# When may the first store start? Splitting the last load of a streaming kernel and releasing two large stores by its landing

## Chip, cores, metric

One core of a Trainium2 chip. The metric is device time in microseconds, median of the runs; all runs told here are with a granted clock of 1.0. Not all ran on one chip: the first four experiments ran on chip 0, the four at 28 and 4, at 10 and 22 rows and with the early whole load on chip 5, the other four on chip 4, each beside runs of before on the same chip (for the first pair the record names no chip). A kernel is best judged by its ratio to before of the same rounds; medians from different chips are compared only roughly. The profile's span is some 1.3 us shorter than the device time of the same execution, so spans are compared with spans and times with times.

## The reference

```python
B, S, D = 1024, 16, 512          # all bf16
def reference(x, y, gamma):      # x, y: [1024, 16, 512], gamma: [512]
    return x + gamma * y
```

That is 16384 rows of 1 KB in each of x, y and the result: 33.6 MB in, 16.8 MB out, one multiply and one add for each element.

## The kernel before

Each of the 128 partitions owns 128 consecutive rows. They are worked in four pieces of 32 rows. SP issues the loads in a fixed order, ACT issues the stores, VectorE multiplies and adds in place in `y_sb`. x has room for two pieces only, so its third and fourth load wait for the first and second add.

```python
PIECES = [32, 32, 32, 32]
X_AT = [0, 32, 0, 32]
X_AFTER = [-1, -1, 0, 1]         # the add that frees the place

SP = [('x', 0), ('y', 0), ('x', 1), ('y', 1), ('y', 2), ('x', 2), ('y', 3), ('x', 3)]
ACT = [('g',), ('s', 0, 0, 2), ('s', 1, 1, 2), ('s', 2, 2, 2), ('s', 3, 3, 3)]
                                  # store, from piece, to piece, after which add
# ... cut ...
    for c in range(n):
        yt = y_sb[:, piece(c), :]
        _take(s_y[c], 16, nc.vector)
        nc.vector.tensor_tensor(out=yt, in0=yt, in1=gamma_sb..., op=MULT).then_inc(s_dve, 1)
        _take(s_x[c], 16, nc.vector)
        _take(s_dve, 1, nc.vector)
        nc.vector.tensor_tensor(out=yt, in0=x_tile(c), in1=yt, op=ADD).then_inc(s_add, 1)
```

All stores, even of the first two pieces, wait for the third add (`2` in the last place). So loads and stores follow one another and hardly overlap.

## Time and profile before

| | |
|---|---|
| time, first three runs | 120.30, 120.31, 120.99 us |
| span of the profiled run | 119.5 us |
| DMA engines | q1 (loads) 66.4% + q10 (stores) 32.5% of the span |
| VectorE | 59% busy, eight passes of 8.69 us |

To read what follows: a *packet* is one record of the profile, here the contiguous run of one partition. A transfer has *landed* when the last of the 16 DMA engines has signalled the end of its part. A line of a *stretch* gives start and end and length in us, the busy time (and number of instructions) of TensorE, its weight load, VectorE and GpSimd, the granted clock, the busy share of the DMA engines and their GB/s. A packet is counted whole in the stretch in which it starts, so the share can pass 1. A line of the *order of time* gives start, duration, engine, line and tiles. The prediction below shows such lines of the kernel before, and why stretches are multiples of the packet time.

### The profile page before, as it was taken

To read this page: it belongs to the slowest core of one execution; us is meant where nothing else is said; L and a number is where in the kernel's file an instruction comes from. 1 tells how busy PE (TensorE), PEld (TensorE's weight loads), DVE (VectorE), ACT (ScalarE), POOL (GpSimd) and SP (SyncE) were. 2 spreads that over 40 slices of the span, in tenths; PEclk is the share of its full clock that TensorE was granted. 3 is DMA by queue.
4 is the path that set the end of the run, shared out by engine and by line. 5 is a ranking of instruction groups with operands and counts; after the bars stand their busy time and mean duration, and the time that the engine had idled before them with its cause. 6 is when DMAs were issued, how large, how long until landed. Compare 5 with 4: busy or idle time off the path is not lost. (4 is left out here: it accounts for less than half of the span.)

```text
span 119.5 us, 84 instructions
## 1 busy us (share of the span) xinstructions
PE 0.6 (0%) x1; PEld 0.1 (0%) x1; DVE 70.2 (59%) x10; POOL 0.2 (0%) x4
## 2 busy tenths in 40 slices
PE   0100000000000000000000000000000000000000
PEld 0000000000000000000000000000000000000000
DVE  0100000699999289999999999999999600000000
POOL 0000000000000000000000000000000000000000
DMA  7989898998998989898989999898989898989995
GB/s 208 494 373 504 351 526 351 384 493 351 384 493 351 526 351 526 351 515 362 493 384 471 406 428 450 384 493 351 526 351 526 351 526 351 515 362 471 406 471 230
DMA packets 1730, 50.33 MB, mean 421 GB/s; under 512 B 193, under 2 KB 194, under 8 KB 194
## 3 DMA queue, kind: packets, MB, share of 16 engines
q1 hardware_dynamic: 1152, 33.55, 66.4%
q10 hardware_dynamic: 578, 16.78, 32.5%
HBM read 33.56 MB, written 16.78 MB: 421 GB/s over the span
## 5 line engine op out<-in xcount | busy, mean ns | idle before, releaser
L115 DVE TENSOR_TENSOR y_sb<-y_sb,gamma_sb 128x16384 bf16<-128x16384 bf16 x4 | 34.8, 8688 | 18.4 <-DVEq L22 18.4
L120 DVE TENSOR_TENSOR y_sb<-x_sb,y_sb 128x16384 bf16<-128x16384 bf16 x4 | 34.8, 8692 | 0.6
L109 DVE CAST gamma_sb<-gamma_ps 128x512 bf16<-128x512 f32 x1 | 0.7, 692 | 3.4 <-DVEq L22 3.4
L104 DVE MEMSET ones_row<- 1x128 bf16 x1 | 0.2, 165 | 2.0 <-PEq L38 2.0
L107 PE MATMUL gamma_ps<-gamma_row,ones_row 1*128 1x512 bf16 x1 | 0.6, 580 | 4.8 <-PEq L22 4.8
L107 PEld LDWEIGHTS gamma_ps<-gamma_row,ones_row 1*128 1x128 bf16 x1 | 0.1, 100 | 4.8 <-issue 4.8
L149 POOL MEMSET const-bfloat16-1.0<- 128x1 bf16 x1 | 0.1, 101 | 0.0
L149 POOL MEMSET const-uint8-127<- 128x1 uint8 x1 | 0.1, 101 | 0.0
L149 POOL MEMSET const-float32-0.0<- 128x1 f32 x1 | 0.1, 98 | 0.2 <-issue 0.2
L149 POOL MEMSET const-float32-1.0<- 128x1 f32 x1 | 0.1, 98 | 0.0
## 6 DMA issues: line engine op xcount, KB each, us to landing
x_sb<-in_x_dram SPq DMA_DIRECT2D x4, 4096.0 KB, 21.5
y_sb<-in_y_dram SPq DMA_DIRECT2D x4, 4096.0 KB, 35.4
out_dram<-y_sb ACTq DMA_DIRECT2D x4, 4096.0 KB, 23.8
gamma_row<-in_gamma_dram ACTq DMA_DIRECT2D x1, 1.0 KB
```

Source lines behind the costliest of these rows:

```text
L104: nc.vector.memset(ones_row, 1.0).then_inc(s_ones, 1)
L107: nc.tensor.matmul(gamma_ps, ones_row, gamma_row, start=True, stop=True).then_inc(s_ps, 1)
L109: nc.vector.tensor_copy(out=gamma_sb, in_=gamma_ps).then_inc(s_dve, 1)
L115: nc.vector.tensor_tensor(out=yt, in0=yt, in1=gamma_sb[:, None, :].to_broadcast([P, PIECES[c], D]), op=MULT).then_inc(s_dve, 1)
L120: nc.vector.tensor_tensor(out=yt, in0=x_tile(c), in1=yt, op=ADD).then_inc(s_add, 1)
L149: nc = _bacc.Bacc("TRN2", target_bir_lowering=False, num_devices=1)
```

## The change

Its intent: the first store may go when most of the last load has landed, so that the engines pass from loads to stores without a gap and without overlap. The last load of x is cut into 22 and 10 rows. TensorE waits for the first part and passes the news to ACT (`s_go`) and to VectorE (`s_rel`). Two stores of 64 rows (64 KB per partition) take the place of four of 32.

```diff
-SP = [('x', 0), ('y', 0), ('x', 1), ('y', 1), ('y', 2), ('x', 2), ('y', 3), ('x', 3)]
-ACT = [('g',), ('s', 0, 0, 2), ('s', 1, 1, 2), ('s', 2, 2, 2), ('s', 3, 3, 3)]
+SP = [('x', 0, 32, 0), ('y', 0, 32), ('x', 32, 64, 32), ('y', 32, 64), ('y', 64, 96), ('x', 64, 96, 0), ('y', 96, 128), ('x', 96, 118, 32), ('x', 118, 128, 54)]
+ACT = [('g',), ('s', 0, 64), ('s', 64, 128)]
+RELEASE = ('x', 96, 118, 32)
 # ... cut: bookkeeping of rows instead of pieces ...
+            if kind == "s" and not went:
+                _take(s_go, 1, eng)
+                went = True
 # ... cut ...
+    _take(s_load[RELEASE], 16, nc.tensor)
+    nc.tensor.sem_inc(s_go, 1)
+    nc.tensor.sem_inc(s_rel, 1)
 # ... cut ...
+                if w == RELEASE:
+                    _take(s_rel, 1, nc.vector)
+                else:
+                    _take(s_load[w], 16, nc.vector)
```

More of the change, by code (lines that the diff above doesn't have):

```diff
@@ L6 @@
 PIECES = [32, 32, 32, 32]
-X_AT = [0, 32, 0, 32]
-X_AFTER = [-1, -1, 0, 1]
-SP = [('x', 0), ('y', 0), ('x', 1), ('y', 1), ('y', 2), ('x', 2), ('y', 3), ('x', 3)]
-ACT = [('g',), ('s', 0, 0, 2), ('s', 1, 1, 2), ('s', 2, 2, 2), ('s', 3, 3, 3)]
-EARLY = [('x', 0), ('y', 0), ('g',)]
+SP = [('x', 0, 32, 0), ('y', 0, 32), ('x', 32, 64, 32), ('y', 32, 64), ('y', 64, 96), ('x', 64, 96, 0), ('y', 96, 128), ('x', 96, 118, 32), ('x', 118, 128, 54)]
+ACT = [('g',), ('s', 0, 64), ('s', 64, 128)]
+EARLY = (2, 1)
+RELEASE = ('x', 96, 118, 32)
+DVE = [('m', 0), ('a', 0), ('m', 1), ('a', 1), ('m', 2), ('a', 2), ('m', 3), ('a', 3)]
 MULT, ADD = mybir.AluOpType.mult, mybir.AluOpType.add
@@ L56 @@
     y_sb = nc.alloc_sbuf_tensor("y_sb", [P, rows, D], dt).ap()
-    x_rows = max(a + r for a, r in zip(X_AT, PIECES))
+    x_loads = [w for w in SP + ACT if w[0] == "x"]
+    y_loads = [w for w in SP + ACT if w[0] == "y"]
+    stores = [w for w in SP + ACT if w[0] == "s"]
+    for loads in (x_loads, y_loads, stores):
+        assert sum(w[2] - w[1] for w in loads) == rows
+    x_rows = max(w[3] + w[2] - w[1] for w in x_loads)
     x_sb = nc.alloc_sbuf_tensor("x_sb", [P, x_rows, D], dt).ap()
@@ L62, with meets, pieces_of, x_at @@
     s_gamma, s_ones, s_ps, s_dve = sem("s_gamma"), sem("s_ones"), sem("s_ps"), sem("s_dve")
-    s_x = [sem(f"s_x{c}") for c in range(n)]
-    s_y = [sem(f"s_y{c}") for c in range(n)]
-    s_add, s_end, s_out = sem("s_add"), sem("s_end"), sem("s_out")
-    def piece(a, b=None):
-        return slice(starts[a], starts[(a if b is None else b) + 1])
-    def x_tile(c):
-        return x_sb[:, X_AT[c] : X_AT[c] + PIECES[c], :]
-    early, stores = [], 0
-    def ring(eng, what, known=-1):
-        nonlocal stores
-        for w in what:
-            kind, args = w[0], w[1:]
-            need = X_AFTER[args[0]] if kind == "x" else args[2] if kind == "s" else -1
+    s_load = {w: sem("s_" + "_".join(map(str, w[:2]))) for w in x_loads + y_loads}
+    s_add, s_go, s_rel, s_end, s_out = sem("s_add"), sem("s_go"), sem("s_rel"), sem("s_end"), sem("s_out")
+    added = [a for kind, *a in DVE if kind == "a"]
+    order = {a[0]: k for k, a in enumerate(added)}
+    def meets(a, b, c, d):
+        return a < d and c < b
+    def pieces_of(a, b):
+        return [c for c in range(n) if meets(starts[c], starts[c + 1], a, b)]
+    def x_at(row):
+        return next(w[3] + row - w[1] for w in x_loads if w[1] <= row < w[2])
+    def frees(w):
+        old = x_loads[: x_loads.index(w)]
+        old = [v for v in old if meets(v[3], v[3] + v[2] - v[1], w[3], w[3] + w[2] - w[1])]
+        return [c for v in old for c in pieces_of(v[1], v[2])]
+    early = []
+    def ring(eng, what, n_early):
+        known, went = 0, False
+        for k, w in enumerate(what):
+            kind = w[0]
+            need = frees(w) if kind == "x" else pieces_of(w[1], w[2]) + list(w[3:]) if kind == "s" else []
+            need = max((order[c] + 1 for c in need), default=0)
+            if kind == "s" and not went:
+                _take(s_go, 1, eng)
+                went = True
             if need > known:
-                eng.wait_ge(s_add, need + 1)
+                eng.wait_ge(s_add, need)
                 known = need
@@ L86, in ring @@
             elif kind == "x":
-                c = args[0]
-                i = eng.dma_start(out=x_tile(c), in_=xv[:, piece(c), :]).then_inc(s_x[c], 16)
+                to = x_sb[:, w[3] : w[3] + w[2] - w[1], :]
+                i = eng.dma_start(out=to, in_=xv[:, w[1] : w[2], :]).then_inc(s_load[w], 16)
             elif kind == "y":
-                c = args[0]
-                i = eng.dma_start(out=y_sb[:, piece(c), :], in_=yv[:, piece(c), :])
-                i.then_inc(s_y[c], 16)
+                r = slice(w[1], w[2])
+                i = eng.dma_start(out=y_sb[:, r, :], in_=yv[:, r, :]).then_inc(s_load[w], 16)
             else:
-                r = piece(args[0], args[1])
+                r = slice(w[1], w[2])
                 i = eng.dma_start(out=ov[:, r, :], in_=y_sb[:, r, :]).then_inc(s_out, 16)
-                stores += 1
-            if w in EARLY:
+            if k < n_early:
                 early.append(i.ins)
-    ring(nc.sync, SP)
-    ring(nc.scalar, ACT)
+    ring(nc.sync, SP, EARLY[0])
+    ring(nc.scalar, ACT, EARLY[1])
     nc.vector.memset(ones_row, 1.0).then_inc(s_ones, 1)
@@ L110, with need @@
     _take(s_dve, 1, nc.vector)
-    for c in range(n):
-        yt = y_sb[:, piece(c), :]
-        _take(s_y[c], 16, nc.vector)
-        nc.vector.tensor_tensor(
-            out=yt, in0=yt, in1=gamma_sb[:, None, :].to_broadcast([P, PIECES[c], D]), op=MULT
-        ).then_inc(s_dve, 1)
-        _take(s_x[c], 16, nc.vector)
-        _take(s_dve, 1, nc.vector)
-        nc.vector.tensor_tensor(out=yt, in0=x_tile(c), in1=yt, op=ADD).then_inc(s_add, 1)
+    _take(s_load[RELEASE], 16, nc.tensor)
+    nc.tensor.sem_inc(s_go, 1)
+    nc.tensor.sem_inc(s_rel, 1)
+    landed, open_mults = set(), 0
+    def need(loads, c):
+        for w in loads:
+            if w not in landed and meets(starts[c], starts[c + 1], w[1], w[2]):
+                if w == RELEASE:
+                    _take(s_rel, 1, nc.vector)
+                else:
+                    _take(s_load[w], 16, nc.vector)
+                landed.add(w)
+    for kind, *args in DVE:
+        c = args[0]
+        yt = y_sb[:, starts[c] : starts[c + 1], :]
+        if kind == "m":
+            need(y_loads, c)
+            g = gamma_sb[:, None, :].to_broadcast([P, PIECES[c], D])
+            nc.vector.tensor_tensor(out=yt, in0=yt, in1=g, op=MULT).then_inc(s_dve, 1)
+            open_mults += 1
+        else:
+            need(x_loads, c)
+            if open_mults:
+                _take(s_dve, open_mults, nc.vector)
+                open_mults = 0
+            at = x_at(starts[c])
+            xt = x_sb[:, at : at + PIECES[c], :]
+            nc.vector.tensor_tensor(out=yt, in0=xt, in1=yt, op=ADD).then_inc(s_add, 1)
     nc.scalar.sem_inc(s_end, 1)
@@ L125 @@
     _take(s_add, n, nc.sync)
-    _take(s_out, 16 * stores, nc.sync)
+    _take(s_out, 16 * len(stores), nc.sync)
     main = nc.main_func.blocks[0].instructions
```

## The prediction

> **What bounds the kernel now**
>
> I read the page first, its engine and queue parts, because a kernel of two elementwise passes over 50 MB is either bound by VectorE or by the DMA engines, and the change touches both.
>
> ```profile
> span 119.5 us, 84 instructions
> PE 0.6 (0%) x1; PEld 0.1 (0%) x1; DVE 70.2 (59%) x10; POOL 0.2 (0%) x4
> ...
> q1 hardware_dynamic: 1152, 33.55, 66.4%
> q10 hardware_dynamic: 578, 16.78, 32.5%
> HBM read 33.56 MB, written 16.78 MB: 421 GB/s over the span
> ```
>
> VectorE works 59% of the span. The load queue q1 and the store queue q10 together fill 66.4 + 32.5 = 98.9% of the 16 DMA engines' time. So the DMA engines are the bound, and the only idle time that is left to win is about 1.1%, or 1.3 us.
>
> The second view is a cut of the span into stretches. A packet here is one partition's 32 KB and takes about 1.21 us, so I chose stretches of about eight packets (one transfer of 4.19 MB); a stretch that does not fit whole packets shows false ups and downs such as those in the 40 slices.
>
> ```profile
> 41.80:51.50 9.70, 0.00 (x0) 0.00 (x0) 9.19 (x2) 0.00 (x0) 1.00 1.00 432
> 51.50:61.20 9.70, 0.00 (x0) 0.00 (x0) 9.70 (x2) 0.00 (x0) 1.00 1.00 432
> 61.20:70.90 9.70, 0.00 (x0) 0.00 (x0) 9.55 (x2) 0.00 (x0) 1.00 1.00 432
> 70.90:80.55 9.65, 0.00 (x0) 0.00 (x0) 9.65 (x2) 0.00 (x0) 1.00 1.01 435
> 80.55:90.20 9.65, 0.00 (x0) 0.00 (x0) 9.50 (x2) 0.00 (x0) 1.00 1.01 435
> 90.20:99.86 9.66, 0.00 (x0) 0.00 (x0) 4.37 (x1) 0.00 (x0) 1.00 1.01 434
> 99.86:109.50 9.64, 0.00 (x0) 0.00 (x0) 0.00 (x0) 0.00 (x0) 1.00 1.01 435
> ```
>
> The last column is GB/s. The reader is to see that loads (up to 80 us) run at 432 and stores (from 80 us) at 435, and that nothing dips between. The handover itself, in stretches of one packet:
>
> ```profile
> 77.60:78.80 1.20, 0.00 (x0) 0.00 (x0) 1.20 (x1) 0.00 (x0) 1.00 1.01 437
> 78.80:80.00 1.20, 0.00 (x0) 0.00 (x0) 1.20 (x1) 0.00 (x0) 1.00 1.01 437
> 80.00:81.20 1.20, 0.00 (x0) 0.00 (x0) 1.20 (x1) 0.00 (x0) 1.00 1.02 437
> 81.20:82.40 1.20, 0.00 (x0) 0.00 (x0) 1.20 (x1) 0.00 (x0) 1.00 1.01 437
> ```
>
> The third view is the order of time around the handover, which says when VectorE and the store issues happen.
>
> ```profile
> 59.72 0.33 SPq L88 DMA_DIRECT2D x_sb<-in_x_dram  x1
> 68.44 8.69 DVE L120 TENSOR_TENSOR y_sb<-x_sb,y_sb 128x16384 bf16<-128x16384 bf16 x1
> 77.05 8.68 DVE L115 TENSOR_TENSOR y_sb<-y_sb,gamma_sb 128x16384 bf16<-128x16384 bf16 x1
> 77.17 4.06 ACTq L95 DMA_DIRECT2D out_dram<-y_sb  x3
> 85.88 8.69 DVE L120 TENSOR_TENSOR y_sb<-x_sb,y_sb 128x16384 bf16<-128x16384 bf16 x1
> ```
>
> The third add ends at 77.05 and releases three stores at 77.17. The trace's single packets complete the picture: the last load packets end between 80.09 and 80.42, engine by engine, and on each engine the first store packet starts within 10 ns of that, after the load's semaphore write. No store packet runs before a load packet. The last store packets end at 118.81 to 119.15 and their landing, 0.36 us later, ends the span. So the chain that counts is: first packet at 0.99 us, 24 load-sized packets less their slow start to 80.1, then 32 store packets of 1.208 us (38.7 us), then 0.36 us of landing. The chain of waits on the page ends at the fourth add and stops there, since it does not follow DMA; it is not the bound.
>
> **What the Trainium skill says**
>
> "DMA: Bandwidth & Descriptors", section "Where 436 GB/s comes from": the 16 ports carry 435.2 GB/s at most. The trace agrees: 432 and 435 above. Store packets of 32768 bytes each took 1213 ns and follow one another every 1.208 us, which is 27.1 GB/s for one engine. There is no rate left to win. The same page, "Issuing engines are not separate DMA queues": transfers from SP and from ACT run on the same 16 engines. The trace agrees, since q1 and q10 share 98.9% of one pool. The same page, "Queues, rings and completion order": each engine takes its rows in turn, a packet at a time. The trace of before neither confirms nor refutes this for the stores, since the first store packet starts exactly where loads end. "Perfetto Trace Analysis", section "DMA Instruction — HWDGE (DVE, Sync)": the issue seen in the profile does not contain the movement. The trace agrees: the first store's issue takes 0.37 us, its first packet starts 2.92 us after the issue starts, and it lands 13.4 us after it.
>
> **The change part by part**
>
> 1. *The front is untouched.* The first eight loads have the same order, sizes and waits (the reuse of x's two halves still waits for the first and second add). Cost 0. The slow start, where the first packets take 1.8 to 2.1 us and not 1.21, stays.
>
> 2. *The last load is split into 22 and 10 rows.* Eight packets of 32 KB per engine become eight of 22 KB (22528 / 27.1 GB/s = 0.83 us) and eight of 10 KB (0.38 us). The bytes are the same. Added: eight packets and one semaphore write of about 10 ns per engine. I give it 0 to 0.1 us.
>
> 3. *Four stores become two.* Packets of 32 KB become packets of 64 KB (if they are not cut in two). A back-to-back store packet costs 1.208 us against 32768 / 27.2 GB/s = 1.205 us at the ceiling, so a packet's own overhead is about 3 ns; 16 packets fewer on each engine give 0.05 us. Two semaphore writes fewer give 0.02 us. Call it -0.05 us.
>
> 4. *The release moves from the third add to a landing.* By the packets, loads end on the engines at 80.09 (earliest) to 80.42 (latest). The 10-row part is the last eight small packets of each engine, 8 x 0.378 = 3.02 us, so the 22-row part ends on the slowest engine at 80.42 - 3.02 = 77.40. In before, the last load landed at 59.72 + 21.1 = 80.84, which is 0.42 us after its last packet. So the part lands at 77.82. TensorE takes a semaphore 0.03 us after it is there and needs 0.05 us for it (its waits of before are 51 ns); two increments and ACT's own take follow. I estimate 0.2 us for the relay, so ACT issues at 78.0, where before it issued at 77.17. The release is 0.85 us *later*, not earlier; the second add, which the first store also needs, is long done (59.7).
>
> 5. *What the handover costs.* In before, 2.92 us pass from issue to first store packet, but the first load at the start of the span needed only 0.99 us. The difference can be a real delay of the path, or the packets already committed on the engine. If it is the second, descriptors arrive at about 79.0, while 10 KB loads still have a microsecond to go: the engines have no gap, and at most a few 64 KB store packets (2.42 us each) slip ahead of the last 10 KB loads. Cost on the engines 0.
>
> 6. *VectorE and the second store.* x's last 10 rows land at 80.84, or 2.4 to 4.8 us later if one or two store packets cut in. The fourth multiply ends at 85.73, so the fourth add still starts at about 85.9 and ends at 94.6, where the second store is issued. The first store's 8.39 MB (16 x 1.208 = 19.3 us) keep the engines busy to 99.4. The second store is there 4.8 us ahead, against 0.99 to 2.9 us that it needs: no gap.
>
> Sum: 0.05 - 0.05 + 0 = 0, so the span stays 119.5 and the time stays at the 120.3 of before.
>
> **The rivals**
>
> *A gap at the handover.* If the 2.92 us are a fixed delay of the path, the first store packet starts at 78.0 + 2.92 = 80.9, and engines idle 0.5 to 0.85 us. The time becomes 120.8 to 121.1. For it: the gamma load, also issued by ACT, needed 2.95 us from issue to packet, nearly the same number. Against it: gamma too waited behind a packet in flight (it began as that packet ended), so it shows only an upper bound. I give this rival 3 in 10.
>
> *A gain from clean separation or larger packets.* If the split keeps loads and stores apart where before mixed them, stores would flow faster. Against it: before did not mix them in its profiled run, and runs at 99 to 100% of the ceiling. In runs that went otherwise (one of the three took 120.99) it might help by some tenths: 120.0.
>
> *The late rows delay VectorE.* If four or more store packets get ahead of the last load packets on some engine, the fourth add starts over 4.9 us late and the second store could leave a gap. Four packets are 9.7 us, so the add ends at 99.4 and the engines run dry for 1 to 3 us: 121.3 to 123.3. At most two or three small loads can be left when the stores arrive, so I give it 1 in 20.
>
> *64 KB runs are cut badly or are slower to HBM.* Nothing in this trace shows a packet over 32 KB. A few per cent on 38.7 us would be over 1 us. I give it 1 in 30.
>
> **Range and chances**
>
> No gap gives 120.3, a gap gives 121.0: 0.7 x 120.3 + 0.3 x 121.0 = 120.5, and the chance of a small gain takes off 0.1. I predict 120.4 us. Before itself spread from 120.3 to 120.99. The range of 119.8 to 121.1 holds both main cases. Within 2% means 117.9 to 122.7: a gain of 2.4 us needs twice the idle time that exists, so faster has 1 in 100; slower needs one of the last two rivals, 3 in 100.
>
> **What would show it**
>
> In stretches of the changed kernel, 432 to 435 GB/s on both sides of 80 us shows steps 2 and 3 right. The first ACT store issue at about 78.0 shows step 4. A stretch without a dip between 78 and 83 us shows step 5; a hole of half a microsecond there, the first rival. The start of the last add at 85.9 shows step 6; a later start with VectorE waiting shows the third rival. A store packet that takes clearly more than 2.42 us would make step 3 wrong. The prediction fails if stores run at another rate than 435 GB/s, or if DMA idles over 1 us anywhere after 5 us.

## The result and the profile after

The changed kernel took 120.12 us (median of 6, 120.08 to 120.14) against 120.46 us of before (median of 6, 120.24 to 120.99). The ratio is 0.9966 with a 95% interval of 0.9944 to 0.9988. Ratios here are the mean time of one kernel's fast runs over that of the other's of the same rounds, so not quite the ratio of the medians. The change is "same" at the 2% level, but the gain of 0.3% is clear of noise, and the changed kernel is steadier.

The page of the changed kernel, its span and queues:

```profile
span 118.8 us, 88 instructions
...
q1 hardware_dynamic: 1296, 33.56, 66.1%
q10 hardware_dynamic: 290, 16.78, 32.6%
HBM read 33.56 MB, written 16.78 MB: 424 GB/s over the span
```

The packets changed as intended (q1 1152 to 1296, q10 578 to 290), and the engines are as full as they were. Loads run at 432 GB/s and stores at 435 as before, which the prediction had named as its first sign (stretches of eight packets, of 32 KB and of 64 KB):

```profile
50.90:60.60 9.70, 0.00 (x0) 0.00 (x0) 9.70 (x2) 0.00 (x0) 1.00 1.00 432
82.00:101.30 19.30, 0.00 (x0) 0.00 (x0) 11.63 (x2) 0.00 (x0) 1.00 1.00 435
```

The order of time around the handover in the changed kernel:

```profile
58.93 0.81 SPq L110 DMA_DIRECT2D x_sb<-in_x_dram  x2
67.65 8.69 DVE L162 TENSOR_TENSOR y_sb<-x_sb,y_sb 128x16384 bf16<-128x16384 bf16 x1
76.26 8.68 DVE L153 TENSOR_TENSOR y_sb<-y_sb,gamma_sb 128x16384 bf16<-128x16384 bf16 x1
77.42 16.73 ACTq L116 DMA_DIRECT2D out_dram<-y_sb  x2
85.09 8.69 DVE L162 TENSOR_TENSOR y_sb<-x_sb,y_sb 128x16384 bf16<-128x16384 bf16 x1
```

The store is issued 1.1 us after the third add (67.65 + 8.69 = 76.34) now and not right behind it. Single packets show the rest: engine by engine the last load packet ends between 79.19 and 79.64, and the first store packet starts within 0.01 us of that. The fourth add follows the multiply without a wait.

But the two profiles can't be subtracted from each other. The 0.7 us between the spans arose much earlier, in code that the change doesn't touch. The same stretches of six packets each, first of before, then of the changed kernel (the last column is GB/s):

```profile
12.10:19.40 7.30, 0.00 (x0) 0.00 (x0) 0.00 (x0) 0.00 (x0) 1.00 1.01 431
19.40:26.70 7.30, 0.00 (x0) 0.00 (x0) 4.64 (x1) 0.00 (x0) 1.00 1.04 417
26.70:34.00 7.30, 0.00 (x0) 0.00 (x0) 7.15 (x2) 0.00 (x0) 1.00 0.90 373
34.00:41.30 7.30, 0.00 (x0) 0.00 (x0) 5.59 (x1) 0.00 (x0) 1.00 1.01 431
```

```profile
12.10:19.40 7.30, 0.00 (x0) 0.00 (x0) 0.00 (x0) 0.00 (x0) 1.00 1.00 431
19.40:26.70 7.30, 0.00 (x0) 0.00 (x0) 4.76 (x1) 0.00 (x0) 1.00 1.00 431
26.70:34.00 7.30, 0.00 (x0) 0.00 (x0) 7.15 (x2) 0.00 (x0) 1.00 1.00 431
34.00:41.30 7.30, 0.00 (x0) 0.00 (x0) 5.47 (x1) 0.00 (x0) 1.00 1.00 431
```

In the profiled run of before the load packets between 15 and 39 us took up to 1.42 us and not 1.21; summed up, 0.9 us for each engine. This "slow stretch" hits some runs and not others. A measure that leaves it out is needed: the time **from the landing of the last y load to the end** (the last landing of a store), in which the whole handover lies. By it, before had 119.51 - 71.12 = 48.39 us and the changed kernel 118.74 - 70.38 = 48.36. By this pair alone the change would do nothing, and the gain of 0.3% would be an accident of slow stretches. The experiments show that this is not the whole truth.

### The profile page after: what moved, and what is told of

Read it like the earlier page. It is cut to its first block, busy times and chain, and to the rows that moved or that the text cites. A ratio compares the mean times of both kernels' runs of the same rounds, so it can differ in the third digit from the quotient of the medians.

```text
span 118.8 us, 88 instructions
## 1 busy us (share of the span) xinstructions
PE 0.6 (0%) x1; PEld 0.1 (0%) x1; DVE 70.2 (59%) x10; POOL 0.2 (0%) x4
## 3 DMA queue, kind: packets, MB, share of 16 engines
q1 hardware_dynamic: 1296, 33.56, 66.1%
```

## The experiments

All outputs are right. The theories: **A**, the gain is chance, from the slow stretch. **B**, one part of the change (release or store size) gains. **C**, the rewritten program text misses the slow stretch. After the first four: **D**, a store issued while loads are still in flight disturbs them, and the landing avoids this by its time. **E**, the small packets of the split load make the handover steady, whoever releases.

### The changed kernel once more

No edit. 

> The changed kernel, unaltered, once more. Theory A (the change is worth under 0.1 us by itself, and the gap of 0.34 us between the medians comes from a slow stretch of load packets that some runs meet between 15 and 39 us, in code that the change does not touch): about 120.1 in most runs, but now and then a run of 120.5 to 121.0 like before. Theory B (the larger stores or the release by a landing make it faster and steadier): 120.1 in every run, before again 120.2 to 121.0. Theory C (the rewritten program, in another order of semaphores and instructions, misses the slow stretch): as B.

Measured: 120.08 us (120.00 to 120.28), before in the same rounds 120.36 (120.14 to 121.20, 11 runs), ratio 0.9965 (0.9938 to 0.9992). The gain repeats. The profiled run, the slowest of them with 120.28, did have a mild slow stretch, so the change doesn't prevent that; C in its strict form falls.

### Only the larger stores

```diff
-... ('x', 96, 118, 32), ('x', 118, 128, 54)]
-ACT = [('g',), ('s', 0, 64), ('s', 64, 128)]
+... ('x', 96, 128, 32)]
+ACT = [('g',), ('s', 0, 64, 2), ('s', 64, 128)]   # first store after the third add
+# no s_go, no s_rel: TensorE's three lines are left out
```

> Only the stores of 64 KB per partition; the last load of x is whole again and the third add releases the first store, as in before. Theory A: the stores gain 0.09 us and the load gains back the 0.1 us of the split, so 120.0 in runs without the slow stretch. Theory B with the release as the cause: 120.3 and more with the spread of before. Theory C: 120.0 in every run.

Measured: 120.39 us (120.01 to 121.10), ratio 0.9993: before's time and before's spread. So store size alone shows no gain, though the interval (0.9958 to 1.0028) is wide. In its trace the store is issued at 76.19, and the load packets that start at 77.34 to 77.67 on all 16 engines take 1.31 to 1.88 us; those that follow take 1.213 again.

### Only the split and the release

```diff
-ACT = [('g',), ('s', 0, 64), ('s', 64, 128)]
+ACT = [('g',), ('s', 0, 32), ('s', 32, 64), ('s', 64, 96), ('s', 96, 128)]
```

> Only the split and the release by the landing; the stores are four of 32 KB per partition again. Theory A: 0.09 us longer than the changed kernel, 120.2. Theory B with the larger stores as the cause: 120.3 and more, with the spread of before. Theory C: 120.2 in every run.

Measured: 120.19 us (120.10 to 120.39), ratio 0.9975 (0.9949 to 1.0002). The gain seems to be largely here, though the interval just reaches 1: of theory B split and release stay. Most of the 0.1 us that it is behind the changed kernel is the larger stores' share (0.08 us by the profiles, see below). From the last y landing to the end it took 48.47 us.

### Neither part, in the new program text

The four stores and the whole last load, the first store after the third add: the schedule of before.

```diff
-... ('x', 96, 118, 32), ('x', 118, 128, 54)]
-ACT = [('g',), ('s', 0, 64), ('s', 64, 128)]
+... ('x', 96, 128, 32)]
+ACT = [('g',), ('s', 0, 32, 2), ('s', 32, 64), ('s', 64, 96), ('s', 96, 128)]
+# no s_go, no s_rel
```

> Neither part: the loads, stores and waits of before, written by the program text of the changed kernel. Theory A: 120.1 to 120.2 where no slow stretch is met, 120.5 to 121.0 where one is, so like before. Theory B: like before, median 120.4, spread of 0.7. Theory C: 120.1 to 120.2 in every run.

Measured: 120.38 us (120.22 to 120.85), ratio 0.9992: before again, so C is out. The profiled run had no slow stretch, so it shows the handover of before's schedule alone. From the last y landing to the end: 48.87 us, 0.40 more than with split and release. The loss is in its load packets between 76.7 and 79.0 us, which took up to 1.81 us. That is theory D: the store was issued at 76.26, with three microseconds of loads ahead. But the first profile of before, issued as early (6.0 us after the last y landing in both), shows no slow packet there. So the loss comes in some runs and not in others.

### The split, but the third add releases

```diff
-ACT = [('g',), ('s', 0, 64), ('s', 64, 128)]
+ACT = [('g',), ('s', 0, 64, 2), ('s', 64, 128)]
+# no s_go, no s_rel
```

> The split of the last load and the stores of 64 KB, but the third add releases the first store again (at about 76.2 us instead of 77.4). Theory D (a store that is issued about 3 us before the loads end disturbs the load packets still in flight and costs 0.3 to 0.7 us in many runs; the release by the landing avoids it by its time): median 120.3 to 120.5, with runs up to 121, like the stores alone. Theory E (the small packets of the split load make the handover steady, whatever releases the stores): 120.1, all runs within 0.2 us.

Measured: 120.22 us (120.11 to 120.47), ratio 0.9995 (0.9972 to 1.0017). Between the two theories' numbers. The profiled run took 48.86 us from the last y landing to the end, as much as without the split, and its 10 KB load packets from 77.96 on took up to 0.67 us and not 0.39, so D for the profile; two of six runs took 120.47, none more. The split alone gains nothing.

### The whole load, the release by the third add but late

```diff
-    _take(s_load[RELEASE], 16, nc.tensor)
-    nc.tensor.sem_inc(s_go, 1)
-    nc.tensor.sem_inc(s_rel, 1)
+    nc.tensor.wait_ge(s_add, 3)
+    for k in range(2):               # about 1 us of idle work
+        late = nc.alloc_psum_tensor(f"late_ps{k}", [P, D], mybir.dt.float32).ap()
+        i = nc.tensor.matmul(late, ones_row, gamma_row, start=True, stop=True)
+    i.then_inc(s_go, 1)
```

The last load is whole, the stores are of 64 KB.

> The last load whole, stores of 64 KB, released by the third add with about 1.1 us of delay (two idle matmuls on TensorE), so that they are issued at about 77.4, as in the changed kernel, with no split and no landing. Theory D: 120.0 to 120.1, nearly as steady as the changed kernel. Theory E: 120.3 to 120.5 with runs up to 121.

Measured: 120.43 us (119.92 to 120.66), ratio 1.0002 (0.9976 to 1.0029). The handover is as D says: the store is issued at 77.47, every load packet after 75 us takes 1.21 to 1.28 us, and the stretch from the last y landing to the end is 48.53 us. But the times are not steady: three of six runs lie at 120.57 to 120.66. The profiled run (120.29) had a mild slow stretch before 70 us; the slower three were not profiled. For the time of a whole run D fails here: with the changed kernel's issue time it is no faster than before, nor than the split with the early release of the same rounds (120.22).

### No split, the landing of the whole load releases

```diff
-... ('x', 96, 118, 32), ('x', 118, 128, 54)]
-RELEASE = ('x', 96, 118, 32)
+... ('x', 96, 128, 32)]
+RELEASE = ('x', 96, 128, 32)
```

> No split: the landing of the whole last load releases the stores. The loads' last packets end at about 79.2 to 79.6, land at 80.1, and the relay takes 0.37 us, so the store is issued at 80.5. If issue to first packet takes 1.77 us, as in the changed kernel, the first store packet starts at 82.3, the engines idle 2.9 us and the time is 122.9. If it takes 0.99 us, as the first load of the span did on idle engines, the gap is 2.1 us and the time is 122.1. If the 2.9 us of before were fixed: 124.0.

Measured: 121.92 us (121.84 to 122.29), ratio 1.0139. The issue in order of time, and the stretches around it:

```profile
80.41 0.37 ACTq L116 DMA_DIRECT2D out_dram<-y_sb  x1
```

```profile
76.80:79.20 2.40, 0.00 (x0) 0.00 (x0) 2.40 (x1) 0.00 (x0) 1.00 0.92 396
79.20:81.20 2.00, 0.00 (x0) 0.00 (x0) 2.00 (x1) 0.00 (x0) 1.00 0.00 0
81.20:83.60 2.40, 0.00 (x0) 0.00 (x0) 2.40 (x1) 0.00 (x0) 1.00 1.02 437
```

The reader is to see the hole: no data packet started between 79.2 and 81.2. The first store packet starts at 81.27, 0.86 us after the issue. So the path from issue to packet costs 0.86 us on idle engines; the rest of the 2.92 us of before and of the 1.77 us of the changed kernel passed while load packets ran on the engines. The split is worth some 1.9 us (50.24 us from the last y landing to the end, against 48.36) *against this way of releasing*.

### The split at 28 and 4 rows: later

```diff
-... ('x', 96, 118, 32), ('x', 118, 128, 54)]
-RELEASE = ('x', 96, 118, 32)
+... ('x', 96, 124, 32), ('x', 124, 128, 60)]
+RELEASE = ('x', 96, 124, 32)
```

> The split moved to 28 and 4 rows, so the release comes later. The last load packets end at 79.2 to 79.6; four rows are 1.21 us of an engine, so the first part lands at about 78.8, the relay of 0.37 us makes it 79.2 for the issue, and with the 0.88 us that the whole landing showed from issue to packet on idle engines the first store packet starts at 80.1. Idle about 0.7 us: 120.7 to 120.8. If the 1.77 us of the changed kernel were the delay: 121.5.

Measured: 120.69 us (120.59 to 120.72), ratio 1.0027. Issue at 79.21, first store packet at 80.08: again 0.86 us, and the gap as worked out. This also fixes the size of the tail: landing to issue (0.35 us) plus issue to packet (0.86 us) plus last packet to landing (about 0.44 us) make 1.7 us; ten rows, 3.1 us of an engine, hide it with something to spare.

### The split at 10 and 22 rows: earlier

```diff
-... ('x', 96, 118, 32), ('x', 118, 128, 54)]
-RELEASE = ('x', 96, 118, 32)
+... ('x', 96, 106, 32), ('x', 106, 128, 42)]
+RELEASE = ('x', 96, 106, 32)
```

> The split moved to 10 and 22 rows, so the release comes early: landing at 73.4, issue at 73.8, store descriptors on the engines at about 74.7 with five to six load packets of 22 KB still to go. If each engine takes turns, a packet from each queue, every one of them waits for a store packet of 2.42 us: the last load lands at 92 to 94, the fourth add ends at 101 to 103, the second store comes 3 to 5 us after the first is through, and the time is 123 to 125. If loads in the queue go first: 120.1. Theory D (stores beside loads disturb the loads) adds 0.5 us or more to either.

Measured: 120.95 us (120.86 to 121.21), ratio 1.0053. Taking turns was seen, but far less came of it. The order of time:

```profile
73.71 23.66 ACTq L116 DMA_DIRECT2D out_dram<-y_sb  x2
76.15 8.69 DVE L153 TENSOR_TENSOR y_sb<-y_sb,gamma_sb 128x16384 bf16<-128x16384 bf16 x1
88.31 8.69 DVE L162 TENSOR_TENSOR y_sb<-x_sb,y_sb 128x16384 bf16<-128x16384 bf16 x1 [3.47 <-DVEq L25]
```

The store was issued at 73.71, but its first packet started at 78.02, 4.31 us later. By then most engines had two load packets of 22 KB left, and each of those did wait for a store packet of 2.42 us. The last load landed at 88.06 and not at 92 to 94, VectorE waited 3.47 us, which cost nothing: the second store was issued at 97.03, just in time. The loss of 0.86 us (49.22 us from the last y landing to the end, against 48.36) lies in load packets between 75 and 78 us, which took up to 1.62 us and not 0.84. Once the queues take turns, both kinds of packets are at full speed (0.836 and 2.418 us).

### The same, with four small stores

```diff
-... ('x', 96, 118, 32), ('x', 118, 128, 54)]
-ACT = [('g',), ('s', 0, 64), ('s', 64, 128)]
-RELEASE = ('x', 96, 118, 32)
+... ('x', 96, 106, 32), ('x', 106, 128, 42)]
+ACT = [('g',), ('s', 0, 32), ('s', 32, 64), ('s', 64, 96), ('s', 96, 128)]
+RELEASE = ('x', 96, 106, 32)
```

> The same early release, but four stores of 32 KB per partition, so a load packet waits for 1.21 us only: the last load lands at about 86 to 87, VectorE ends within 1.5 us of its usual time and the engines never run dry. What is left is the cost of mixing itself. Theory D, in which stores beside loads slow the load packets: 120.7 or more, with packets of 22 KB clearly over 0.84 us in the trace between 74 and 87. If mixing is free: 120.2.

Measured: 121.00 us (120.93 to 121.49), ratio 1.0061. The last load landed at 84.56, VectorE was not late, the engines never ran dry, and still 0.8 us and more are lost. The load packets of 22 KB between 75 and 78 us took up to 1.83 us; those after 79 us, beside store packets, 0.836. So D holds with a correction: not the mixing costs, but what comes before it. The slow load packets start between 75.0 and 77.8 us, after the issue (73.69) and before the first store packet (78.50). VectorE isn't the reason: its fourth multiply starts at 76.1 to 76.3 us in the changed kernel too, where no load packet is slow.

### The same, with a whole load

```diff
-... ('x', 96, 118, 32), ('x', 118, 128, 54)]
-ACT = [('g',), ('s', 0, 64), ('s', 64, 128)]
-RELEASE = ('x', 96, 118, 32)
+... ('x', 96, 128, 32)]
+ACT = [('g',), ('s', 0, 32), ('s', 32, 64), ('s', 64, 96), ('s', 96, 128)]
+RELEASE = ('y', 96, 128)
 ...
-    nc.tensor.sem_inc(s_go, 1)
+    # s_go comes from the last of 7 idle matmuls, about 3 us later
```

> The same with whole loads of 32 KB packets: the landing of the last y load, plus about 3 us of idle matmuls on TensorE, releases four stores of 32 KB at about 73.9; the packets of both queues are of one size. If engines take turns, the last load lands at about 85.5 and VectorE is not late. Theory D: 120.7 or more, with load packets over 1.22 us between 74 and 86. Theory E (small packets of the split make the handover steady): this one is slower than the split one with the same release by 0.2 us or more. If mixing is free: 120.2 to 120.3.

Measured: 120.93 us (120.75 to 121.19), ratio 1.0048. As slow as with the split, so the split does not protect against an early release, and E falls in this form. The stretches of two packets, first of this kernel (issue at 73.84), then of the whole load with the late release (issue at 77.47):

```profile
73.00:75.40 2.40, 0.72 (x2) 0.00 (x0) 2.40 (x1) 0.00 (x0) 1.00 1.02 437
75.40:77.80 2.40, 0.00 (x0) 0.00 (x0) 2.40 (x2) 0.00 (x0) 1.00 1.06 314
77.80:80.20 2.40, 0.00 (x0) 0.00 (x0) 2.40 (x1) 0.00 (x0) 1.00 0.98 423
80.20:82.60 2.40, 0.00 (x0) 0.00 (x0) 2.40 (x1) 0.00 (x0) 1.00 0.98 423
```

```profile
73.00:75.40 2.40, 0.00 (x0) 0.00 (x0) 2.40 (x1) 0.00 (x0) 1.00 1.03 437
75.40:77.80 2.40, 1.03 (x2) 0.13 (x2) 2.40 (x2) 0.00 (x0) 1.00 1.02 437
```

The second line of the first fence is the loss: 2.4 us x (1 - 314/437) = 0.68 us. In single packets: those that started at 75.65 to 75.94 took 1.67 to 2.17 us and not 1.21. Over all load packets from 74 us on it is 0.85 us for each engine, and that is all that this kernel is behind split and landing with the same stores (49.34 against 48.47). The share of busy time in that line is full (1.06), since a slow packet counts as busy: only the GB/s column shows it. The first store packet starts at 78.92, in the third line; in the fourth each engine's last load packet takes its turn between store packets, in 1.213 us.

### A version meant to beat both

```diff
-SP = [('x', 0, 32, 0), ('y', 0, 32), ('x', 32, 64, 32), ('y', 32, 64), ('y', 64, 96), ('x', 64, 96, 0), ('y', 96, 128), ...]
+SP = [('y', 0, 64), ('x', 0, 64, 0), ('y', 64, 128), ('x', 64, 96, 0), ...]     # rest as changed; frees() goes by rows
-DVE = [('m', 0), ('a', 0), ('m', 1), ('a', 1), ('m', 2), ('a', 2), ('m', 3), ('a', 3)]
+DVE = [('m', 0), ('m', 1), ('a', 0), ('a', 1), ('m', 2), ('m', 3), ('a', 2), ('a', 3)]
```

> A version meant to beat both: as the changed kernel, but rows 0 to 64 of y and of x and rows 64 to 128 of y are loaded with 64 KB per partition each, and VectorE's order is adapted. If load packets of 64 KB gain what store packets gained (1.2137 to about 1.2086 us for each 32 KB), 48 of the 64 load packets of an engine gain 0.25 us: 119.85. If the load rate is set by HBM reads and not by packets: 120.1. If VectorE's new order makes the second store late: over 120.3.

Measured: 120.19 us (119.95 to 120.29, 5 runs), ratio 0.9983 (0.9959 to 1.0008). In the trace a load of 64 rows took 19.32 and 19.35 us where two of 32 took 19.43, so larger load packets do gain some 0.1 us a pair, but between 66 and 78 us this run lost 0.2 us in slow load packets. The changed kernel did not run on this chip, so whether this one beats it is open.

### All of them on one scale

The first column of numbers is when the first store was issued, counted from the landing of the last y load, from each profiled run. Counted the same way, the last load packets end at about 9 us when nothing disturbs them. The second is the time from that landing to the end.

| kernel | issue, us | to the end, us | median time, us | ratio to before of its rounds (chip) |
|---|---|---|---|---|
| 10/22, two stores | 3.43 | 49.22 | 120.95 | 1.0053 (5) |
| 10/22, four stores | 3.45 | 49.89 | 121.00 | 1.0061 (5) |
| whole, early, four stores | 3.54 | 49.34 | 120.93 | 1.0048 (5) |
| whole, third add, two stores | 5.57 | 49.12 | 120.39 | 0.9993 (0) |
| split, third add, two stores | 5.99 | 48.86 | 120.22 | 0.9995 (4) |
| before's schedule in the new text | 6.01 | 48.87 | 120.38 | 0.9992 (0) |
| before (its profiled run) | 6.05 | 48.39 | 120.32 (39 runs) | 1 |
| changed kernel | 7.04 | 48.36 | 120.12 | 0.9966 (not recorded) |
| split, landing, four stores | 7.07 | 48.47 | 120.19 | 0.9975 (0) |
| whole, third add late | 7.07 | 48.53 | 120.43 | 1.0002 (4) |
| changed kernel, once more | 7.15 | 48.48 | 120.08 | 0.9965 (0) |
| 28/4 | 8.88 | 49.03 | 120.69 | 1.0027 (5) |
| whole, landing | 10.06 | 50.24 | 121.92 | 1.0139 (4) |

In these profiles too early costs 0.5 to 1.5 us (slow load packets), too late costs a gap, and about 7 us is the floor of the valley. Of the seven with the issue at 6.05 us or earlier, six have slow load packets between 75 and 79.5 us, 0.16 to 1.04 us for each engine if summed up. The six with the issue at 7.04 or later have 0.06 us at most. The one that doesn't fit is the profiled run of before: at 6.05 it shows no disturbed packet at all.

## Why the prediction was right

The time (120.4 predicted, 120.12 measured) lay in the range, in its lower half. A range of 1.3 us holds no gain and the measured one alike, so this alone says little. The prediction also set a span (119.5) and a time (120.3) side by side that come from different runs: the run with that span took 120.87. By its steps:

1. *The front is untouched*: right for the code, but for two slips in counting: seven loads stay as they were, the eighth is the one that is split; and before the stores each engine moves 64 load packets (eight loads of 128 packets over 16 engines), not 24. That its duration would not vary by run was an assumption, and wrong by up to 0.9 us.
2. *The split costs 0 to 0.1 us*: from the last y landing to the last x landing the changed kernel took 9.78 us and the whole load, undisturbed, 9.71. So 0.08 before rounding: right.
3. *Two stores instead of four, -0.05 us*: 38.58 us against 38.66 from the last x landing to the end, so -0.08: right in kind and nearly in size.
4. *The release comes later*: right. Relay 0.35 us and not 0.2 (each of TensorE's three semaphore steps came 0.15 us after the one before it); issue at 77.42 and not 78.0, since the loads themselves were 0.7 us earlier than in the slow run that the estimate was built on. (The 77.05 that it gives for the end of the third add is the start of the next multiply; the add's line ends at 68.44 + 8.69 = 77.13.)
5. *The handover costs 0*: the handover of the changed kernel is free, as said, and the path needs 0.86 us when idle (the whole landing and 28/4 show it), so "descriptors after 1 us" was nearly right, and the first rival, a fixed 2.9 us, is refuted. **The term that was mis-sized is the other side of this step.** The sum took before's handover as free too, because its one profiled run showed no disturbed packet, and so the second rival (separation) got "some tenths" in runs that went otherwise and 0.1 us in the number. Of the two profiles of before's schedule one shows no loss (48.39) and one, in the new text, 48.87 against 48.47 with split and release: 0.40 us, in a run that met it. In the medians it is 0.19 us (120.38 and 120.19).
6. *VectorE and the second store*: right. The fourth add started at 85.09 behind the multiply, and the second store was issued at 93.81.

Third rival, late rows: what it needs was made on purpose with 10/22, and even then VectorE's 3.47 us of waiting did not reach the end. Fourth, runs of 64 KB slower: refuted, 2.418 us a packet.

What is shown: split and landing together put the issue where neither a gap nor a disturbance occurs, and an issue 3.5 us earlier costs some 0.8 us in three kernels alike (0.5 to 0.6% above before of their rounds, where the changed kernel is 0.3% below). What is argued only: that the gain of 0.3% over before is this avoided loss, since the right issue time alone, with the whole load, did not gain (1.0002). Why an issue slows loads in flight isn't shown by any run. What stays open: why the late release of a whole load, with a clean handover in its profile, had three of six runs over 120.5, when of the 18 runs with split and landing (both runs of the changed kernel and that with four stores) none was over 120.45, and of before 12 of 39 were. A landing moves with the loads when a slow stretch delays them, and the third add does so only in part; that would fit, but none of those slow runs was profiled to show it. Nor did the changed kernel run on chip 4, where the late release of the whole load and the split alone were tried. The source of the slow stretches is open as well.

## What to carry to other kernels

Where loads hand over to stores, look for the best moment of the first store's issue. In this kernel the path takes 1.2 us from landing to packet; the best releases measured came some 2.5 us before the loads ran dry (landing at 77.1, last load packets at 79.6), those of 73.4 and of 78.9 were worse. Tie it to the landing of a late part of the load stream; that this is better because it moves with the stream is a guess here. Don't subtract two profiles when a run can lose more to chance than the change is worth: find a landmark after the chance event and compare from there, and build the old schedule in the new text as a control. And read GB/s beside the busy share, because a slowed packet looks busy.

## What the Trainium skill lacked or had wrong

- "DMA: Bandwidth & Descriptors", section "Latency and other measured facts", gives about 600 ns for the first byte on this path. From the start of the issue to the first packet the runs show 0.86 us on idle engines (twice), 0.99 us for the first load, and 1.77 to 5.07 us with loads in flight. The page has the first kind only.
- The same page, "Queues, rings and completion order", has each engine take its rows in turn by packets, which there are groups of some 9 to 17 descriptors. The runs with the early release show turns, of single runs of one partition: the last one or two load packets of most engines alternate with store packets (load and store 1.213 us each with the whole load). But the first store packet came 4.3 to 5.1 us after the issue, behind three or more load packets of each engine.
- No page has the cost of starting a store stream beside loads in flight: with the early whole load 0.85 us for each engine, in load packets of 32 KB of up to 2.17 us and not 1.21. They come before the first store packet; the 16 load packets that run between store packets afterwards take 1.213 us.
- No page has the slow stretches of load packets in some runs (373 GB/s and not 431 for 7 us, with no store in flight).
- No page says what a larger packet gains above 32 KB: 64 KB against 32 KB made 38.7 us of stores 0.08 us shorter.
